# Half of the score spreads moved from SP's queue to GpSimd's, first values loaded earlier, mixing weights built earlier

## The chip, the cores and the metric

The kernel runs on one core of a Trainium2 chip. A core has a matrix engine (TensorE, PE in the profile), three engines for elementwise work (VectorE or DVE, ScalarE or ACT, GpSimd or POOL), SyncE (SP), which here only issues transfers, and 16 DMA engines that carry out the transfers of all queues. The metric is the time of one launch in microseconds of the device.

## What is computed

The reference is a talking-heads attention followed by two feed-forward blocks, in float32. Cut to what matters:

```python
# batch 2, 12 heads, 448 positions, head size 64
scores = q @ k^T / 8                                 # per head
scores = einsum('bhij,hg->bgij', scores, w_pre)      # mix the heads
attn   = softmax(scores)                             # over j
attn   = einsum('bhij,hg->bgij', attn, w_post)       # mix again
x      = (attn @ v), heads side by side              # 896 x 768
x = (h * clip(h + 3, 0, 6) / 6) @ w_out    with h = x @ w_in     # 768 -> 2048 -> 768
x = (P(h) / Q(h)) @ w_out2                 with h = x @ w_in2    # P cubic, Q quadratic
```

## The kernel before

**Tiles.** The 896 query rows are cut into eight chunks (`chunks`, four for each batch), six of them of 120 rows and two of 88 (the last of a batch, carried as 100). A chunk's rows form 12 groups of 10 rows (10 groups in the short chunks), and a step of the main loop (line 506) takes two groups. Scores are made for one head at a time with the chunk's rows on the partitions (`scores`, line 214, matrix product at L225). A mix over heads needs the heads on the partitions: for each group, 5 rows times 12 heads make 60 partitions, and two such halves lie at partitions 0 and 64. So each head's scores, once copied from PSUM into a staging tile (`stg`, five buffers, L230), are rearranged within the core by DMA into the tile `full` of the chunk (two buffers). This is the **spread**: two transfers a head of 60 rows of 448 floats (105 KB), 24 a chunk (line 197, issue at L201). For chunks 0 and 1 all heads are staged first (`stage`, `stage1`), and the spreads go by group instead of by head, 24 a chunk as well (`spread_group`, line 204, L206), so that the first group can be mixed before the last has come.

**A step** of the main loop does, for pair m of groups: `premix(m)`, the first mix on TensorE (M, L245), a row maximum on VectorE (L251) and the exponential on ScalarE (L253); `postmix(m - 2)`, the second mix (A, L287), which also normalizes, as its weights `wr` were divided by the row sums; the scores of the next chunk, two head pairs in each of the steps 0 to 2 (`SST`); the product of attention and values of the chunk before, X (L310, `av_unit`), two head pairs in each of the steps 3 to 5, or three in each of the steps 3 and 4 where the chunk itself has five steps (`AVST`; `AVLAST` in the last chunk); the copies; and `norm(m)` (line 258), where VectorE inverts the row sums and GpSimd multiplies them into the weights `wr` (L263). A wr is read by the `postmix` two steps later.

**The order** is the program's own: from line 436 on the schedule is written by hand, and each engine and each DMA queue works off its instructions in the order of the code. All DMAs but two go through SP's queue. It holds, in this order, the loads of keys and queries, chunk 0's spreads by group (L444), chunk 1's (from step 3 of chunk 0, L510), the first four loads of values (step 4, L513), and then for each chunk the 24 spreads in the order of the heads and the loads of values. There are four buffers for values (`vraw`), each for a pair of heads. `av_unit` issues the load four pairs ahead when it has emitted the products of a pair (L314); so pairs 4 and 5 of a chunk are loaded when pairs 0 and 1 have been used, in the same chunk's turn. Each transfer signals its landing by a semaphore, of which SP's queue uses eight in turn.

`build_mix` (line 179) makes, on GpSimd, the weights of both mixes (`wp`, `wq`) from the tiny loaded matrices.

**After the attention** come the two feed-forward blocks. Their weights are loaded, unpacked and split into two parts on ScalarE and VectorE ahead of the matrix products (h, y, acc at L331 to L333), which take three passes each. The first products h begin within the last chunk's steps (L566).

Of the kernel before, what the change touches and what calls it, by code (L numbers as in the profile page):

```python
# [22 lines left out]
HR = GR // 2  # L23
# [23 lines left out]
def fused_kernel(  # L47
# [15 lines left out]
    nc = tc.nc  # L63
# [49 lines left out]
    def load_q(C):  # L113
        ns = chunks[C][3] * GR
        t = front.tile([128, NP, CH], F32, tag="qraw", bufs=3, name=f"qraw{C}")
        nc.sync.dma_start(out=t[:, :, :ns], in_=q[C, :, :, :ns])
        qraw[C] = t

    def load_k(b, hp):
        if hp == 0:  # L120
            keys[b] = front.tile([128, NP, S], F32, tag="keys", bufs=2, name=f"keys{b}")
        nc.sync.dma_start(out=keys[b][:, hp], in_=k[b, :, hp])

    def load_v(C, hp):
        if C < len(chunks) - 1:
            t = att.tile([JP, 2, JC * D], F32, tag="vraw", bufs=4, name=f"vraw{C}_{hp}")
            nc.sync.dma_start(out=t, in_=v[chunks[C][0], hp])
            vraw[(C, hp)] = t
# [22 lines left out]
    for i, w in enumerate((w_pre, w_post)):  # L151
        for a in range(0, 128, 64):
            nc.sync.dma_start(
                out=wrep[a : a + HP, i, :], in_=w[None, :, :].to_broadcast([HR, H, H])
# [16 lines left out]
    def load_ab():  # L171
        nc.sync.dma_start(out=pa, in_=p_a.partition_broadcast(128))
        nc.sync.dma_start(out=pb, in_=p_b.partition_broadcast(128))

    def build_ab():
        nc.scalar.activation(out=pb, in_=pb, func=AF.Abs)
        nc.vector.tensor_scalar(out=pa, in0=pa, scalar1=-1.0, scalar2=None, op0=ALU.mult)

    def build_mix():
        w = wp[:, :HP].rearrange("p (i g) -> p i g", g=H)  # L180
        nc.gpsimd.tensor_tensor(
            out=w,
            in0=mask[:, :, None].to_broadcast([128, HR, H]),
            in1=wrep[:, 0, None, :].to_broadcast([128, HR, H]),
            op=ALU.mult,
        )
        nc.gpsimd.tensor_scalar(out=w, in0=w, scalar1=float(D) ** -0.5, scalar2=None, op0=ALU.mult)
        nc.gpsimd.tensor_tensor(
            out=wq,
            in0=wrep[:, 1, :, None].to_broadcast([128, H, HR]),  # L190
            in1=mask[:, None, :].to_broadcast([128, H, HR]),
            op=ALU.mult,
        )
# [2 lines left out]

    def spread(C, h, st):
        n = chunks[C][3]
        for a in range(2):
            to = full[C][64 * a : 64 * a + HP].rearrange("(i h) g s -> h i g s", h=H)[h]  # L200
            nc.sync.dma_start(out=to[:, :n], in_=st[a * HR * n : (a + 1) * HR * n])  # L201

    def spread_group(C, g, st):
        n = chunks[C][3]
        for a in range(2):
            nc.sync.dma_start(  # L206
                out=full[C][64 * a : 64 * a + HP, g, :],
                in_=st[a * HR * n : (a + 1) * HR * n].rearrange("(i g) h s -> g i (h s)", g=n)[g],
            )
# [4 lines left out]
    def scores(C, hp, tag="sc", st=None):  # L214
        n = chunks[C][3] * GR
        b = chunks[C][0]
        if hp == 0:
            full[C] = att.tile([128, MG, S], F32, tag="full", bufs=2, name=f"full{C}")
        sc = [ps.tile([128, 512], F32, tag=tag, bufs=BUFS[tag], name=f"sc{C}_{2 * hp + i}") for i in range(2)]
        far = st is None  # L220
        if far:
            st = front.tile([CH, 2, S], F32, tag="raw", bufs=5, name=f"stg{C}_{hp}")
        for i in range(2):
            o = slice(i * D, i * D + D)
            nc.tensor.matmul(  # L225
                sc[i][:n, :S], lhsT=qraw[C][o, hp, :n], rhs=keys[b][o, hp], start=True, stop=True
            )

        def take(i, copy):
            copy(out=st[:n, i], in_=sc[i][:n, :S])  # L230
            if far:
                spread(C, 2 * hp + i, st[:, i])

        return [lambda copy: take(0, copy), lambda copy: take(1, copy)]
# [4 lines left out]
    def premix(m):  # L239
        C, g = pairs[m]  # L240
        mt = [ps.tile([128, 512], F32, tag="M", bufs=BUFS["M"], name=f"M{m}_{a}") for a in range(2)]
        for a in range(2):
            for c in range(2):
                o = slice(64 * a, 64 * a + HP)
                nc.tensor.matmul(  # L245
                    mt[a][64 * c : 64 * c + 64, :S], lhsT=wp[o], rhs=full[C][o, g + c, :], start=True, stop=True
                )
        st = att.tile([128, 8], F32, tag="st", bufs=5, name=f"st{m}")
        e = att.tile([128, 2, S], F32, tag="e", bufs=3, name=f"e{m}")
        for a in range(2):  # L250
            nc.vector.tensor_reduce(out=st[:, a : a + 1], in_=mt[a][:, :S], op=ALU.max, axis=AX.X, negate=True)  # L251
        for a in range(2):
            nc.scalar.activation(  # L253
                out=e[:, a], in_=mt[a][:, :S], func=AF.Exp, bias=st[:, a : a + 1], accum_out=st[:, 2 + a : 3 + a]
            )
        epx[m] = (e, st)
# [162 lines left out]
    def load_units(i):  # L419
        while ucur[0] < len(units) and ucur[0] <= i:  # L420
            load_unit(units[ucur[0]])
            ucur[0] += 1
# [17 lines left out]
    for hp in range(NP):  # L440
        ev = scores(0, hp, "sc" if hp % 3 else "M", stage[:, 2 * hp : 2 * hp + 2])
        ev[0](acopy)
        ev[1](vcopy)
    for g in range(chunks[0][3]):  # L444
        spread_group(0, g, stage)
    build_mix()

    for hp in range(FIRST):
        ev = scores(1, hp, st=stage1[:, 2 * hp : 2 * hp + 2])
# [53 lines left out]
    for C, (b, r0, n, G) in enumerate(chunks):  # L503
        nxt = C + 1 if C + 1 < len(chunks) else None
        G //= 2
        for s in range(G):
            if C and C + 2 < len(chunks) and s == (3 if C == 1 else 0):
                load_q(C + 2)
            if C == 0 and s == 3:
                for g in range(chunks[1][3]):  # L510
                    spread_group(1, g, stage1)
                XL = xp.tile([128, KD, NT], F32R, tag="xl", name="xl")
            if C == 0 and s == 4:  # L513
                for i in range(4):
                    load_v(0, i)
            if C == 2 and s >= 3:
                load_k(1, 2 * s - 6)
                load_k(1, 2 * s - 5)
            if C == 2 and s == 1:
                load_ab()  # L520
            if C == 3 and s == 0:
                build_ab()
            premix(m)
            for p in later:
                p()
            later.clear()
            sc, xs = [], []
            if m >= LAG:
                postmix(m - LAG)
            if nxt is not None and not C:  # L530
                if s < NP - FIRST:
                    sc += scores(nxt, FIRST + s, st=stage1[:, 2 * FIRST + 2 * s : 2 * FIRST + 2 * s + 2])
            elif nxt is not None:
                for hp in range(NP):
                    if SST[hp] == s:
                        sc += scores(nxt, hp)
            if C:
                for i, t in enumerate(AVST[G] if nxt is not None else AVLAST):
                    if t == s:
                        xs += av_unit(C - 1, 2 * i + 1)  # L540
            for p in sc[:-1]:
                p(vcopy)
            if m >= LAG:
                at_evac(m - LAG, acopy)
            for p in sc[-1:]:
                p(acopy)
            for p in xs[::2]:
                p()
            later += xs[1::2]
            norm(m)  # L550
            if C == PRE and s == LATE - 1:
                front.release()
                pools["late"] = tc.alloc_tile_pool(name="late", bufs=1, side="right", reuse_waits="tile")
                load_units(1)
                wpieces = (p for u in units[:4] for p in split_pieces(u))
            if C == PRE and s == G - 1:
                pieces(1)
            if C > PRE:
                pieces(2)
            if C > PRE and s == 1:  # L560
                load_vs()
            if C > PRE and s == 2:
                load_units(2)
            if nxt is None and s >= 3:
                if s == 3:
                    h100 = gemm1(0, 0, ps.tile([128, 512], F32, tag="sc", bufs=BUFS["sc"], name="h1_0_0"))  # L566
                for _ in range(3):
                    next(h100)
            m += 1

    C = len(chunks) - 1
# [315 lines left out]
```

## Time and profile before

| | |
|---|---|
| median of 3 runs | 764.01 us (761.32 to 765.96) |
| the profiled execution | 762.19 us, its span 760.4 us |
| TensorE busy | 666.9 us, 88% of the span |
| VectorE, ScalarE busy | 502.7 us (66%), 383.8 us (50%) |
| GpSimd busy | 32.1 us (4%) |
| mean granted clock of TensorE | 0.942 |
| DMA queue of SP | 122.94 MB, 50.7% of 16 engines' span |

The span runs from the first to the last instruction; the execution's own time has some 1.8 us around it. Times in rows are microseconds from the start of the span unless marked ns. PE is a matrix product, PEld a weight load beside it; SPq is SP's sequencer, which issues transfers. `full<-stg` is a transfer or instruction that writes the tile `full` and reads `stg`. An arrow to the left behind an idle time names what ended it. The granted clock is given as a share of full speed: 1.00 is 2.4 GHz, 0.50 is 1.2 GHz.

### The profile page before, as it was taken

To read this page: it belongs to the slowest core of one execution; us is meant where nothing else is said; L and a number is where in the kernel's file an instruction comes from. 1 tells how busy PE (TensorE), PEld (TensorE's weight loads), DVE (VectorE), ACT (ScalarE), POOL (GpSimd) and SP (SyncE) were. 2 spreads that over 40 slices of the span, in tenths; PEclk is the share of its full clock that TensorE was granted. 3 is DMA by queue.
4 is the path that set the end of the run, shared out by engine and by line. 5 is a ranking of instruction groups with operands and counts; after the bars stand their busy time and mean duration, and the time that the engine had idled before them with its cause. 6 is when DMAs were issued, how large, how long until landed. Compare 5 with 4: busy or idle time off the path is not lost.

```text
span 760.4 us, 16385 instructions
## 1 busy us (share of the span) xinstructions
PE 666.9 (88%) x6682; PEld 558.0 (73%) x6682; DVE 502.7 (66%) x860; ACT 383.8 (50%) x701; POOL 32.1 (4%) x67
## 2 busy tenths in 40 slices
PE   8966485565749599999999999999999999999998
PEld 2434253343436468988988888888999999999997
DVE  4442162434435265989999855553999899999991
ACT  4643162435445364555565333322766667669861
POOL 1100010001000042000000000000000000000000
PEclk9996696868788899999999999999999999999999
DMA  5343528343442674756665533332765766574622
GB/s 176 123 146 119 147 94 201 121 123 131 118 148 93 198 215 130 229 170 215 213 194 187 160 110 112 111 126 103 253 214 201 240 221 249 168 257 149 200 92 84
DMA packets 77055, 124.35 MB, mean 164 GB/s; under 512 B 6804, under 2 KB 57268, under 8 KB 76980
## 3 DMA queue, kind: packets, MB, share of 16 engines
q1 hardware_dynamic: 76692, 122.94, 50.7%
q8 instruction: 53, 0.87, 0.5%
q10 hardware_dynamic: 288, 0.37, 0.1%
q14 instruction: 22, 0.18, 0.1%
HBM read 84.24 MB, written 19.27 MB: 136 GB/s over the span
## 4 chain that ended last, share of the span: by engine, by line
PE 79%; DMA 11%; SPq 3%; ACT 3%; DVE 2%; issue 1%; POOL 0%; ACTq 0%; DVEq 0%; POOLq 0%
PE h L331 10%; PE h L332 10%; PE h L333 10%; DMA vraw<-in_v_dram 6%; PE M L245 5%; PE X L310 5%; PE y L331 5%; PE y L333 5%; PE acc L331 5%; PE acc L332 5%; PE acc L333 5%; PE y L332 5%; PE sc L225 4%; PE A L287 3%; DMA full<-stage 3%; ACT e L253 2%
## 5 line engine op out<-in xcount | busy, mean ns | idle before, releaser
L331 PE MATMUL h<-xh,wh 128*128 128x512 f32 (+1 forms) x384 | 140.4, 366 | 0.0
L332 PE MATMUL h<-xl,wh 128*128 128x512 f32 (+1 forms) x384 | 140.3, 365 | 0.0
L333 PE MATMUL h<-xh,wl 128*128 128x512 f32 (+1 forms) x384 | 139.2, 363 | 0.0
L251 DVE TENSOR_REDUCE st<-M 128x1 f32<-128x448 f32 x92 | 53.8, 620 | 114.7 <-PE M L245 111.5
L310 PE MATMUL X<-at,vraw 120*64 120x120 f32 (+1 forms) x672 | 49.1, 313 | 79.4 <-DMA vraw<-in_v_dram 79.3
L310 PEld LDWEIGHTS X<-at,vraw 120*64 120x64 f32 x672 | 43.8, 169 | 81.6 <-DMA vraw<-in_v_dram 72.0
L253 ACT ACTIVATE e<-M,st 128x448 f32<-128x448 f32 x92 | 57.6, 630 | 55.7 <-DVE st L251 55.5
L331 PEld LDWEIGHTS h<-xh,wh 128*128 128x128 f32 x384 | 72.2, 188 | 8.2 <-issue 0.2
L333 PEld LDWEIGHTS h<-xh,wl 128*128 128x128 f32 x384 | 72.2, 188 | 8.0
L332 PEld LDWEIGHTS h<-xl,wh 128*128 128x128 f32 x384 | 72.3, 188 | 6.6
L406 ACT ACTIVATE wh<-wf 128x768 fp32r<-128x768 f32 (+1 forms) x52 | 42.5, 818 | 60.6 <-PE y L332 48.2
L379 ACT ACTIVATE wf<-wraw 128x768 f32<-128x768 f32 (+1 forms) x56 | 49.5, 884 | 46.6 <-DVE wl L407 44.1
L333 PE MATMUL y<-gh,wl 128*128 128x384 f32 x192 | 70.7, 368 | 0.0
L331 PE MATMUL y<-gh,wh 128*128 128x384 f32 x192 | 70.5, 367 | 0.0
L407 DVE TENSOR_TENSOR wl<-wf,wh 128x768 fp32r<-128x768 f32 (+1 forms) x52 | 48.0, 923 | 33.9 <-ACT wh L406 33.9
L332 PE MATMUL y<-gl,wh 128*128 128x384 f32 x192 | 70.0, 364 | 0.0
L245 PE MATMUL M<-full,wp 60*64 60x448 f32 x368 | 62.6, 596 | 6.9 <-ACT e L253 6.6
L287 PEld LDWEIGHTS A<-wr,e 60*56 60x56 f32 x2944 | 50.4, 130 | 24.3 <-issue 19.2
L383 DVE SCALAR_TENSOR_TENSOR wf<-wraw,icst,wf 128x768 int32<-128x768 int32 (+1 forms) x56 | 55.2, 987 | 1.0
L387 DVE SCALAR_TENSOR_TENSOR wf<-wraw,icst,wf 128x768 int32<-128x768 int32 (+1 forms) x56 | 55.2, 985 | 0.7
L287 PE MATMUL A<-wr,e 60*56 60x60 f32 x2944 | 52.1, 218 | 1.0 <-ACT at L295 1.0
L323 ACT ACTIVATE xh<-X 128x240 fp32r<-128x240 f32 (+1 forms) x24 | 8.7, 365 | 80.5 <-PE X L310 80.5
(96 smaller groups left out, 1182.4 us busy)
## 6 DMA issues: line engine op xcount, KB each, us to landing
wraw<-in_moe_w_out_dram SPq DMA_DIRECT2D x28, 768.0 KB
wraw<-in_moe_w_in_dram SPq DMA_DIRECT2D x22, 768.0 KB
vraw<-in_v_dram SPq DMA_DIRECT2D x42, 240.0 KB
full<-stg SPq DMA_DIRECT2D x96, 105.0 KB
wpre<-in_moe_w_in_dram SPq DMA_DIRECT2D x10, 768.0 KB
w2h<-wh SPq DMA_DIRECT2D x16, 384.0 KB
w2l<-wl SPq DMA_DIRECT2D x16, 384.0 KB
ws<-w2h SPq DMA_DIRECT2D x16, 384.0 KB
```

The costliest lines, as they stand in the source:

```text
L245: nc.tensor.matmul(mt[a][64 * c : 64 * c + 64, :S], lhsT=wp[o], rhs=full[C][o, g + c, :], start=True, stop=True)
L251: nc.vector.tensor_reduce(out=st[:, a : a + 1], in_=mt[a][:, :S], op=ALU.max, axis=AX.X, negate=True)
L253: nc.scalar.activation(out=e[:, a], in_=mt[a][:, :S], func=AF.Exp, bias=st[:, a : a + 1], accum_out=st[:, 2 + a : 3 + a])
L287: nc.tensor.matmul(av[64 * c : 64 * c + JH, r, jc, :, a * HR : a * HR + HR], lhsT=e[o, a, j : j + JH], rhs=wr[o, a], start=True, stop=True,)
L310: nc.tensor.matmul(X[hh % 2 * D : hh % 2 * D + D, hh % 4 // 2, :n], lhsT=vs[:, jc, :], rhs=at[C][:, jc, hh, :n], start=(jc == 0), stop=(jc ...
L331: nc.tensor.matmul(o, lhsT=wh, rhs=mh, start=first, stop=False)
L332: nc.tensor.matmul(o, lhsT=wh, rhs=ml, start=False, stop=False)
L333: nc.tensor.matmul(o, lhsT=wl, rhs=mh, start=False, stop=last)
L379: nc.scalar.activation(out=w, in_=hw.bitcast(F32), func=AF.Copy, scale=2.0**-112)
L383: nc.vector.scalar_tensor_tensor(out=wi, in0=hw, scalar=icst[:, 0:1], in1=wi, op0=ALU.bitwise_and, op1=ALU.bitwise_or)
L387: nc.vector.scalar_tensor_tensor(out=wi, in0=lw, scalar=icst[:, 1:2], in1=wi, op0=ALU.logical_shift_right, op1=ALU.bitwise_or)
L407: nc.vector.tensor_tensor(out=lv, in0=w, in1=hv.bitcast(F32), op=ALU.subtract)
```

## The change

Of the two transfers that spread a head's scores (or a group's), the first stays in SP's queue and the second goes into GpSimd's. `build_mix` is emitted before the spreads of chunk 0 instead of after them. The first four loads of values are emitted in step 1 of chunk 0, behind its `premix`, instead of in step 4 ahead of it.

```diff
@@ -196,14 +196,14 @@
 
     def spread(C, h, st):
         n = chunks[C][3]
-        for a in range(2):
+        for a, eng in enumerate((nc.sync, nc.gpsimd)):
             to = full[C][64 * a : 64 * a + HP].rearrange("(i h) g s -> h i g s", h=H)[h]
-            nc.sync.dma_start(out=to[:, :n], in_=st[a * HR * n : (a + 1) * HR * n])
+            eng.dma_start(out=to[:, :n], in_=st[a * HR * n : (a + 1) * HR * n])
 
     def spread_group(C, g, st):
         n = chunks[C][3]
-        for a in range(2):
-            nc.sync.dma_start(
+        for a, eng in enumerate((nc.sync, nc.gpsimd)):
+            eng.dma_start(
                 out=full[C][64 * a : 64 * a + HP, g, :],
                 in_=st[a * HR * n : (a + 1) * HR * n].rearrange("(i g) h s -> g i (h s)", g=n)[g],
             )
@@ -441,9 +441,9 @@
         ev = scores(0, hp, "sc" if hp % 3 else "M", stage[:, 2 * hp : 2 * hp + 2])
         ev[0](acopy)
         ev[1](vcopy)
+    build_mix()
     for g in range(chunks[0][3]):
         spread_group(0, g, stage)
-    build_mix()
 
     for hp in range(FIRST):
         ev = scores(1, hp, st=stage1[:, 2 * hp : 2 * hp + 2])
@@ -510,9 +510,6 @@
                 for g in range(chunks[1][3]):
                     spread_group(1, g, stage1)
                 XL = xp.tile([128, KD, NT], F32R, tag="xl", name="xl")
-            if C == 0 and s == 4:
-                for i in range(4):
-                    load_v(0, i)
             if C == 2 and s >= 3:
                 load_k(1, 2 * s - 6)
                 load_k(1, 2 * s - 5)
@@ -521,6 +518,9 @@
             if C == 3 and s == 0:
                 build_ab()
             premix(m)
+            if C == 0 and s == 1:
+                for i in range(4):
+                    load_v(0, i)
             for p in later:
                 p()
             later.clear()
```

## Rows read from the trace of the kernel before

**Rows 1.** Busy time by stretch: length, then PE, PEld, DVE, ACT, POOL; clock, DMA share, GB/s.

```profile
60.00:290.00 230.00, 151.50 (x3528) 106.43 (x3526) 93.06 (x227) 99.58 (x228) 23.64 (x44) 0.82 0.48 140
290.00:760.40 470.40, 466.73 (x2472) 428.78 (x2470) 383.29 (x573) 257.02 (x416) 3.41 (x3) 1.00 0.54 177
```

**Rows 2.** Waits before 300 us: us in total, times, longest us.

```profile
PE X L310 <- DMA vraw<-in_v_dram: 79.3, 7, 14.0
PE M L245 <- ACT e L253: 6.6, 3, 4.6
...
DVE stg L230 <- DMA full<-stg: 16.2, 2, 15.9
```

**Rows 3.** Chain of waits, 136 to 165 us: start us, us, what.

```profile
145.02 0.60 SPq L201
...
150.15 8.05 DMA vraw<-in_v_dram
```

**Rows 4.** SP's queue in order of time: start us, us, line, transfer, count.

```profile
10.21 38.68 SPq L206 DMA_DIRECT2D full<-stage  x48
...
49.05 4.49 SPq L127 DMA_DIRECT2D vraw<-in_v_dram  x4
...
138.04 12.02 SPq L201 DMA_DIRECT2D full<-stg  x14
```

**Rows 5.** SP's issues by tile: ns min/median/max, first and last start us.

```profile
L201 SPq DMA_DIRECT2D full<-stg x144: 712/732/1016, 54.8 to 254.4; - x144
...
L127 SPq DMA_DIRECT2D vraw<-in_v_dram x42: 324/330/1053, 49.1 to 274.5; - x42
```

**Rows 6.** DMA, 141 to 149 us, then 150 to 158: packets, MB, share; 40 slices.

```profile
q1 hardware_dynamic: 560, 0.93, 32.4%
...
DMA  3333339539998999986979999987633333322324
...
q1 hardware_dynamic: 798, 1.40, 67.5%
```

**Rows 7.** TensorE in order of time, 158 to 175 us and 210 us: start us, us.

```profile
158.25 3.47 PE L310 MATMUL X<-at,vraw 120*64 120x120 f32 x32 [13.99 <-DMA vraw<-in_v_dram]
...
161.64 1.77 PE L245 MATMUL M<-full,wp 60*64 60x448 f32 x8
...
166.37 0.98 PE L245 MATMUL M<-full,wp 60*64 60x448 f32 x8
167.18 1.02 PE L287 MATMUL A<-wr,e 60*56 60x60 f32 x64
...
170.67 1.06 PE L287 MATMUL A<-wr,e 60*56 60x60 f32 x64
...
210.38 1.86 PE L310 MATMUL X<-at,vraw 120*64 120x120 f32 x32
```

**Rows 8.** VectorE and GpSimd, 165 to 169 us: start us, us, idle before.

```profile
165.72 1.69 DVE L230 COPY stg<-sc 120x448 f32<-120x448 f32 x3 [0.42 <-PE sc L225]
...
167.86 0.39 POOL L263 TENSOR_TENSOR wr<-wq,st 128x120 f32<-128x120 f32 x1 [22.29 <-DVE st L261]
```

**Rows 9.** Groups by line: busy us, mean ns, idle before it.

```profile
L404 POOL TENSOR_TENSOR wl<-wf,wh 128x768 fp32r<-128x768 f32 x4 | 7.4, 1843 | 0.3
...
L407 DVE TENSOR_TENSOR wl<-wf,wh 128x768 fp32r<-128x768 f32 (+1 forms) x52 | 48.0, 923 | 33.9 <-ACT wh L406 33.9
```

**Rows 10.** First two chunks, GpSimd and TensorE in order of time: start us, us.

```profile
26.99 0.39 POOL L263 TENSOR_TENSOR wr<-wq,st 128x120 f32<-128x120 f32 x1 [4.02 <-DVE st L261]
...
23.24 0.43 PE L287 MATMUL A<-wr,e 60*56 60x60 f32 x12
...
34.03 0.43 PE L287 MATMUL A<-wr,e 60*56 60x60 f32 x12
...
39.22 1.77 PE L225 MATMUL sc<-keys,qraw 64*120 64x448 f32 x8
...
58.73 3.40 PE L310 MATMUL X<-at,vraw 120*64 120x120 f32 x32 [8.58 <-DMA vraw<-in_v_dram]
```

## The prediction

> **What bounds the kernel now.** I read four views in this order. First the busy time by stretch [rows 1]: from 290 us to the end TensorE is busy 466.73 of 470.40 us at a clock of 1.00, and the change touches nothing there. Between 60 and 290 us it is busy 151.50 of 230 us at a mean clock of 0.82, so what can be won lies there, in the attention. Then TensorE's waits [rows 2]: of its idle time before 300 us, 79.3 us in 7 waits of up to 14.0 us are products X (attention times values) waiting for the load of vraw; another 6.6 us, one wait of 4.6 among them, are mixes M behind a late exponential. Third, the chain through one of the seven [rows 3]: from 145.02 us it runs along SP's spreads at L201, at 150.15 us it changes to a vraw load, and that takes 8.05 us to land. So the wait has two halves: 5 us in which the load stands behind spreads in SP's queue, and 8 us of transfer.
>
> Fourth, both halves by themselves. **The queue:** SP issues 24 spreads a chunk at a median of 732 ns where a vraw load takes 330 [rows 5], and with the gaps 0.81 to 0.86 each: 14 of them take 12.02 us, and chunks 0 and 1 take 38.68 us for 48 [rows 4]. **The transfer:** where only spreads run, their packets take 32.4% of the 16 DMA engines, which is 5.2 engines' work [rows 6], 560 packets or 9.3 spreads of 60 rows in 8 us, 0.86 us each. So a spread keeps about five engines busy, and these serve hardly faster than SP issues. When the vraw loads come, the line of 40 slices goes from 3 to 9 tenths and falls back to 3 before the loads are in [rows 6]: eleven engines have finished and five still work off the spreads ahead of the loads.
>
> **The change, part by part.** Twelve of a chunk's 24 spreads go to GpSimd's queue; SP saves 12 x 0.81 = 9.7 us a chunk. TensorE's step with scores is 3.5 us long (A to A, 167.18 to 170.67 [rows 7]), four heads fall into it, and SP's four remaining issues, 3.2 us, fit in. So SP is no longer behind when the X of a chunk begin, and the load for head pair 4, which waits for the X of pair 0 to free its buffer, goes out at once. It has two steps less half an X, 7.0 - 0.9 = 6.1 us, until it is needed. Its transfer was 8.05 us behind the backlog; with fewer spreads ahead I take 7 us, and leave 1 us of each of the seven waits: 79.3 - 7 = **72.3 us less**. The five-step chunk has less room than that, which the 1 us is to cover on the mean.
>
> The wait of 4.6 us at M stems from the same backlog: just before it VectorE's copy of scores waits 15.9 us for a staging buffer whose spread has not landed [rows 2]. **4.6 less**. After each wait TensorE also works at the low level, 1.2 GHz: at 158 us X takes 3.47 us where it takes 1.86 later, and M 1.77 where it takes 0.98 [rows 7], 2.4 us here. I take 2 for each of seven: **14 less**. In all 90.9 us.
>
> Against it stand GpSimd's costs. No row shows a DMA issued by GpSimd; call its price p. The nearest row from below is SP's own issue of this transfer, 0.73 us [rows 5]. On one and the same subtraction GpSimd takes 1843 ns where VectorE takes 923 [rows 9], 2.0 times as long; by that p would be 1.46 at most. I take **1.0**: between the two, nearer to SP's row, which is the same transfer. GpSimd's slowest instruction, 1.84 us, is the outer bound. The Trainium skill (DMA: Bandwidth & Descriptors, Latency and other measured facts) gives about 1 us to the first byte on this path against 0.6 on SP's; by that alone the sum would be the same.
>
> GpSimd's queue is in order, and behind the spreads stands wr, the weights that each second mix A needs. In a step with scores the first copy is done at about 166.4 us, wr runs at 167.86 for 0.39, and the A that reads it starts at 170.67 [rows 7, 8]: 2.4 us to spare. With four spreads ahead of it, wr ends at 166.4 + 4p + 0.4, so at p = 1.0 it is 0.1 us late; the next two steps each add 4p + 0.4 - 3.5 = 0.9. That is 1.9 us a chunk, in general 12p - 10.1, over six chunks: **11.4 more**.
>
> In the first two chunks it is coarser. Chunk 0's twelve run from 10.2 to 22.2 us, and wr for step 0 comes at 22.6, in time for its A at 23.24 [rows 10]. Chunk 1's twelve stand ahead of step 3's wr. They begin when the third wr is through, 27 us, and end at 39; the A of step 3, at 34.03 before, follows at 39.4, and the scores of chunk 2, at 39.22 before, at some 42.4: **3 more**. These scores were held up by spreads before too, so little of the 5 us shows.
>
> **The early load of the first values** moves four issues of SP, 330 ns each, from 49.05 us [rows 4] to behind chunk 0's twelve, about 20 us, and ahead of chunk 1's twelve, which wait for the copies of step 2's scores anyway. So nothing queues behind them for long. Its gain, the 8.58 us that the X of 58.73 us waits [rows 10], is one of the seven waits and counted there. If chunk 1's halves on SP came 1.5 us later, the 39.4 us of GpSimd would cover it. **The mixing weights ahead of the spreads** cost nothing: they must be there before the first M, and GpSimd would otherwise make them twelve spreads later, some 12 us.
>
> Sum: 762.2 (this execution: span 760.4 and 1.8 around it) - 90.9 + 11.4 + 3 = 685.7. The median of the runs stands 1.8 us above this execution, so **687**.
>
> **Rivals.** (a) *The same five engines.* If GpSimd's spreads run on the engines that SP's use, the transfers don't get faster. A chunk's 24 spreads need 24 x 0.86 = 20.6 us of them and TensorE asks for them within three steps, 10.5 us. When the load for pair 4 is issued, about half of SP's twelve are still ahead of it, sharing the engines with as many of GpSimd's, some 10 us; it lands about 5 us after it is needed instead of 1. With 4.5 us in each of six chunks, 27 in all, the time is 714. For it speaks that a transfer of the same shape takes five engines now [rows 6]; against it that no row says which five GpSimd would take. The Trainium skill speaks against the change here (DMA: Bandwidth & Descriptors, Rules for kernel authors): spreading DMAs over SP, ACT and GpSimd gives no bandwidth and only saves issue time. The same page (Why a DMA increments its semaphore by 16 and not by 1) has GpSimd's transfers begin at an engine that moves on from one to the next, where SP's take the lowest-numbered. No row here decides between the two.
>
> (b) *A dearer issue*, p = 1.5: 12p - 10.1 = 7.9 us a chunk, 47, and 9 in chunk 1; with the 90.9 that leaves 34.5 of gain, 729.
>
> (c) *GpSimd's queue becomes the bound, and the kernel slower.* In each chunk TensorE then waits at A for wr, three steps in a row. The loss 6 x (12p - 10.1) + 3 + 12(p - 1) meets the 90.9 at p = 1.91; from there it decides. At p = 2.2 it is 115, and the time 788. For it speaks that wr has 2.4 us of room and that GpSimd has taken up to twice another engine's time; against it that 1.91 is above every row of GpSimd's and 2.6 times SP's own issue.
>
> (d) *It does nothing that shows:* the loads stay late for another reason, as SP's queue waits for X to free buffers anyway, and 764 stands. Against it: in the chain of rows 3 the load is preceded by spreads alone, not by an X.
>
> **How the numbers follow.** My forecast 0.60 (665 to 705: p from 0.73 to 1.2, and a rest of 0 to 1 us at each wait), (a) 0.13, (b) 0.13, (c) 0.10, (d) 0.04. Faster by more than 0.5%, about the least that a measurement of this kernel tells from no change, is the forecast with (a) and (b): 0.86; the same 0.04; slower 0.10. The low end, 665, is p = 0.73 with no wait left; the high end, 735, takes in (a) and (b). What stays out is (c), (d) and the tails of the others, 0.2.
>
> **What would show it.** Right: TensorE's waits for vraw fall from 79.3 us to under 15; SP's line shows 12 spreads a chunk with the vraw load right after an X; GpSimd has 96 DMA issues of about 1.0 us each; TensorE's clock between 60 us and the end of the attention is near 1.00, and the stretch in which TensorE hardly waits any more starts near 214 us instead of 290 [rows 1]; A waits for wr some 2 us a chunk. Rival (a): the DMA share where spreads run alone stays at a third, and X still waits several us a chunk. (b) and (c): GpSimd's issues take 1.5 us or 2 us and more, and A waits for wr in three steps of every chunk. The forecast is wrong if p is over 1.3, or if another engine (VectorE, which copies, reduces and normalizes in each step) sets the step as soon as TensorE no longer waits.

## The result, and the profile after

The changed kernel takes 727.09 us (median of 4 runs, 725.2 to 730.83) against 764.91 for the kernel before beside it (4 runs): a ratio of 0.952, 95% interval 0.947 to 0.957. That is faster and within the range, but the gain is 37.8 us where some 77 was forecast. The profiled execution took 725.2 us, its span 723.4, 37.0 less than the one before.

The first view again is busy time by stretch, columns as in [rows 1]; the second row cuts the attention at 255 us, behind its last long wait:

```profile
60.00:290.00 230.00, 184.17 (x3744) 134.76 (x3735) 119.24 (x262) 114.77 (x250) 61.64 (x104) 0.90 0.61 164
...
60.00:255.00 195.00, 149.17 (x3531) 103.57 (x3523) 90.33 (x220) 97.68 (x222) 58.95 (x102) 0.88 0.61 161
```

The attention is shorter, but not dense: from 60 to 255 us TensorE is idle for 46 of 195 us, at a mean clock of 0.88. The waits before 300 us say what for (us in total, times, longest us); they answer to [rows 2]:

```profile
PE X L310 <- DMA vraw<-in_v_dram: 41.0, 7, 9.1
...
PE A L287 <- POOL wr L263: 4.7, 2, 4.3
...
PE M L245 <- ACT e L253: 3.2, 4, 1.2
PE M L245 <- DMA full<-stage: 3.0, 2, 2.2
```

X still waits 41.0 us for vraw, where 7 was forecast. A waits for wr almost only once. So GpSimd's side went better than forecast and SP's worse. The issues by tile (ns min/median/max; first and last start) show both, against [rows 5]:

```profile
L201 SPq DMA_DIRECT2D full<-stg x72: 712/802/2561, 47.4 to 214.3; - x72
L201 POOL DMA_DIRECT2D full<-stg x72: 573/582/632, 47.7 to 212.2; - x72
L206 SPq DMA_DIRECT2D full<-stage x24: 721/1124/3073, 10.1 to 45.2; - x24
L206 POOL DMA_DIRECT2D full<-stage x24: 573/593/792, 10.8 to 39.6; - x24
```

An issue costs GpSimd 0.58 us, less than SP. SP's own issues of the same transfers have grown: by head from 0.73 to 0.80 us in the median, by group from 0.74 to 1.12, and the longest of all from 1.02 to 3.07. What that does to a value load is seen in the two queues in order of time, first GpSimd's and then SP's, while one chunk's scores are spread (start us, us):

```profile
110.33 2.43 POOL L201 DMA_DIRECT2D full<-stg  x4 [11.47 <-DMA qraw<-in_q_dram]
...
113.95 2.43 POOL L201 DMA_DIRECT2D full<-stg  x4 [0.78 <-DVE stg L230]
...
117.40 2.55 POOL L201 DMA_DIRECT2D full<-stg  x4 [0.61 <-DVE stg L230]
```

```profile
110.06 15.31 SPq L201 DMA_DIRECT2D full<-stg  x12
125.46 11.20 SPq L127 DMA_DIRECT2D vraw<-in_v_dram  x6
```

GpSimd issues its half of a head as soon as the copy is done, the last four at 117.40 to 119.95. SP's halves of the same four heads, ready just as early, go out until 125.4: the single issues there take 2.22, 1.83, 0.96 and 0.94 us. SP is held by its issues, not by data. Nor do its eight semaphores hold it: the one that each of these four issues takes in its turn had its earlier landing complete 3.7 to 4.7 us before. TensorE in order of time beside it:

```profile
119.12 2.68 PE L310 MATMUL X<-at,vraw 120*64 120x120 f32 x48
...
123.60 1.04 PE L310 MATMUL X<-at,vraw 120*64 120x120 f32 x16
132.83 3.47 PE L310 MATMUL X<-at,vraw 120*64 120x120 f32 x32 [8.19 <-DMA vraw<-in_v_dram]
136.23 1.77 PE L245 MATMUL M<-full,wp 60*64 60x448 f32 x8
```

The first 16 of the products at 119.12 use head pair 0; they end at 120.2 and free the buffer that pair 4's load needs. Had SP kept pace with GpSimd, it would have been through by then; it issues that load at 125.46. TensorE wants the values at 124.6 and gets them at 132.8. The chain of waits through that place has the same three pieces (start us, us):

```profile
124.88 0.48 SPq L201
...
125.46 7.23 DMA vraw<-in_v_dram
...
132.83 3.47 PE X L310 x32
```

**Each wait taken apart.** From single products and issues of the trace I worked out, for pair 4 of a chunk, how long after its buffer came free the load was issued (late), how long from the issue to the X that used it (transit), and how long TensorE had other work from the freeing on (room). Late plus transit less room is the wait. Means over X of the first six chunks, in us:

| kernel | late | transit | room | wait |
|---|---|---|---|---|
| before | 11.5 | 7.6 | 7.3 | 11.8 |
| after | 5.1 | 8.0 | 6.3 | 6.8 |
| forecast for after | 0 | 7 | 6.1 | 1 |

Transit and room were forecast nearly right. The lateness was to vanish, and only halved.

### The profile page after: what moved, and what is told of

It is laid out like the page before. It is cut to its first block, busy times and chain, and to the rows that moved or that the text cites. A ratio compares the mean times of both kernels' runs of the same rounds, so it can differ in the third digit from the quotient of the medians.

```text
span 723.4 us, 16553 instructions
## 1 busy us (share of the span) xinstructions
PE 663.3 (92%) x6682; PEld 555.0 (77%) x6682; DVE 502.5 (69%) x860; ACT 383.4 (53%) x701; POOL 88.6 (12%) x163
## 4 chain that ended last, share of the span: by engine, by line
PE 84%; DMA 9%; issue 3%; ACT 1%; SPq 1%; POOL 1%; DVE 1%; POOLq 0%; ACTq 0%; DVEq 0%
PE h L331 11%; PE h L332 11%; PE h L333 11%; DMA vraw<-in_v_dram 6%; PE y L331 5%; PE y L333 5%; PE acc L331 5%; PE acc L332 5%; PE acc L333 5%; PE y L332 5%; PE X L310 5%; PE M L245 5%; PE sc L225 5%; PE A L287 4%; DMA full<-stage 2%
## 5 line engine op out<-in xcount | busy, mean ns | idle before, releaser
L253 ACT ACTIVATE e<-M,st 128x448 f32<-128x448 f32 x92 | 57.5, 629 | 60.3 <-DVE st L251 60.3
L310 PE MATMUL X<-at,vraw 120*64 120x120 f32 (+1 forms) x672 | 46.4, 302 | 41.0 <-DMA vraw<-in_v_dram 41.0
L310 PEld LDWEIGHTS X<-at,vraw 120*64 120x64 f32 x672 | 41.2, 160 | 43.0 <-issue 41.3
L245 PE MATMUL M<-full,wp 60*64 60x448 f32 x368 | 56.5, 621 | 6.2 <-ACT e L253 3.2
L201 POOL DMA_DIRECT2D full<-stg x72 | 42.4, 589 | 83.9 <-DVE stg L230 52.7
```

Source lines behind the costliest of these rows:

```text
L245: nc.tensor.matmul(mt[a][64 * c : 64 * c + 64, :S], lhsT=wp[o], rhs=full[C][o, g + c, :], start=True, stop=True)
L253: nc.scalar.activation(out=e[:, a], in_=mt[a][:, :S], func=AF.Exp, bias=st[:, a : a + 1], accum_out=st[:, 2 + a : 3 + a])
L310: nc.tensor.matmul(X[hh % 2 * D : hh % 2 * D + D, hh % 4 // 2, :n], lhsT=vs[:, jc, :], rhs=at[C][:, jc, hh, :n], start=(jc == 0), stop=(jc ...
```

## The experiments

All ratios are against the kernel before, run on the same chip; it took 762.6 to 763.9 us in these sessions. The edits are shortened to what matters: `...` stands for lines or arguments left out, and remarks behind `#` are not in the code. Two readings of the late loads stood against each other after the result. P: GpSimd's transfers share engines with SP's, whose transfers therefore crawl and hold SP's issues, and the loads stand behind them. Against it: the loads are late whatever queue they stand in, or GpSimd's issuing as such slows SP's.

### What is left without GpSimd's queue

```diff
-        for a, eng in enumerate((nc.sync, nc.gpsimd)):
+        for a, eng in enumerate((nc.sync, nc.sync)):      # in spread and spread_group
```

> The changed kernel with both halves of every spread on SP, so that only the early load of the first values and the mixing weights ahead of the spreads are left of the change. If the gain is GpSimd's queue nearly alone, as the two undone parts (2 and 3 us, each inside the noise) say: 755 to 765 us, X waits still 65 us or more, SP's issues of spreads back at a median of 0.73 us. Rival (the parts need each other, or the early load carries a large share of the gain): under 750 us.

763.58 us (12 runs), ratio 1.001 (0.9986 to 1.0033). X waits in six places instead of seven and M, behind two kinds of releaser, for 13.4 us instead of 6.6:

```profile
PE X L310 <- DMA vraw<-in_v_dram: 72.2, 6, 14.2
PE M L245 <- ACT e L253: 10.1, 3, 8.1
PE M L245 <- DMA full<-stage: 3.3, 4, 1.5
```

So the early load and the early weights give nothing that shows by themselves: what X gains there M loses. The gain comes with GpSimd's queue. This run is also the cleanest look at what that queue does to SP, as no X is near in the first 50 us. SP's queue there, both halves on SP (start us, us):

```profile
10.40 19.32 SPq L206 DMA_DIRECT2D full<-stage  x24
29.77 2.39 SPq L127 DMA_DIRECT2D vraw<-in_v_dram  x4
32.27 21.36 SPq L206 DMA_DIRECT2D full<-stage  x24
```

and in the changed kernel:

```profile
10.10 15.74 SPq L206 DMA_DIRECT2D full<-stage  x12
25.88 3.01 SPq L127 DMA_DIRECT2D vraw<-in_v_dram  x4
30.48 16.02 SPq L206 DMA_DIRECT2D full<-stage  x12
```

Half the spreads take 81% and 75% of the time: 0.81 and 0.89 us each alone, 1.31 and 1.34 beside GpSimd's. The forecast had counted 0.81.

### The two small parts undone, one at a time

The loads of the first values back at their old place:

```diff
-            if C == 0 and s == 1:      # behind premix
+            if C == 0 and s == 4:      # ahead of premix
                 for i in range(4):
                     load_v(0, i)
```

> The changed kernel with the first four loads of values back in step 4 of chunk 0, behind chunk 1's spreads. If the early load is worth its old wait (8.6 us before the X of 58.7 us), a wait of 5 to 9 us comes back at chunk 1's first X and the time is 731 to 736; if what follows swallows it, the time stays within 725 to 729.

728.92 us, ratio 0.956 (0.951 to 0.961): 2 us from the changed kernel, inside the intervals. And the weights behind the spreads again:

```diff
-    build_mix()
     for g in range(chunks[0][3]):
         spread_group(0, g, stage)
+    build_mix()
```

> The changed kernel with the mixing weights made behind chunk 0's spreads again. GpSimd then makes them when its twelve issues are through, at about 20 us instead of 8 to 9, and the first M starts at about 21 us instead of 13.8: 6 to 8 us more, 733 to 735, if nothing later swallows it; 727 if it does.

730.42 us, ratio 0.957 (0.951 to 0.963). The waits show what the move prevents:

```profile
PE M L245 <- POOL wp L187: 7.6, 1, 7.6
```

but most of these 7.6 us were swallowed later; the time differs by 3 us, and that is not resolved.

### The second half on ScalarE's queue

```diff
-            eng.dma_start(out=to[:, :n], in_=st[a * HR * n : (a + 1) * HR * n])
+            x, y = to[:, :n], st[a * HR * n : (a + 1) * HR * n]
+            if a:
+                held_s.append((x, y))
+            else:
+                nc.sync.dma_start(out=x, in_=y)
...                                       # at the end of the step:
             later += xs[1::2]
+            for x, y in held_s:
+                nc.scalar.dma_start(out=x, in_=y)
+            held_s.clear()
```

> The second half of every chunk's spreads by head goes to ScalarE's queue instead of GpSimd's (issued at the end of the step; the first two chunks' spreads by group stay as in the changed kernel). Theory E (GpSimd's transfers run on other DMA engines than SP's, and that is where the gain comes from): ScalarE's spreads sit on the same five engines as SP's, the DMA share where spreads run alone stays near a third (0.33 to 0.40), X still waits 70 us or more in all, and the time is 745 to 785, the upper end from ScalarE's own 12 issues of 0.73 us a chunk. Theory I (only SP's issue time counts, whoever takes the other half): X waits some 41 us as in the changed kernel, and the time is 727 to 745.

745.69 us, ratio 0.976 (0.972 to 0.980). X waits only 6.9 us, for another reason than either side had named: ScalarE was late. Its exponentials stand behind its own issues, and these behind landings. The group of the exponentials (busy us, mean ns, idle before and what ended it):

```profile
L257 ACT ACTIVATE e<-M,st 128x448 f32<-128x448 f32 x92 | 57.6, 630 | 115.5 <-DMA full<-stg 57.5 <-DVE st L255 36.0 <-DVE stg L234 21.7
```

M then waits 36.5 us for e in all. But one thing is plain here. In stretches in which both queues only carry spreads the DMA share (the last but one column) is that of SP alone [rows 6]:

```profile
120.00:125.00 5.00, 3.91 (x80) 1.77 (x78) 3.20 (x7) 2.63 (x6) 0.39 (x1) 1.00 0.34 119
125.00:130.00 5.00, 1.54 (x8) 0.43 (x6) 1.69 (x3) 0.56 (x2) 0.00 (x0) 1.00 0.33 120
```

In the changed kernel, in the chunk shown above (the third row is the wait of X, for later):

```profile
112.00:116.00 4.00, 4.00 (x88) 2.24 (x86) 3.41 (x8) 3.01 (x7) 3.11 (x7) 1.00 0.58 152
116.00:120.00 4.00, 4.00 (x98) 2.42 (x95) 3.21 (x8) 2.92 (x8) 3.17 (x7) 1.00 0.72 172
128.00:132.00 4.00, 0.00 (x0) 0.00 (x0) 0.00 (x0) 0.00 (x0) 0.00 (x0) 0.50 0.91 224
```

ScalarE's spreads run on the engines that SP's use, five of 16; GpSimd's bring other engines in. The Trainium skill (DMA: Bandwidth & Descriptors, Rules for kernel authors) holds that spreading DMAs over SP, ACT and GpSimd gives no bandwidth; the trace agrees for SP with ScalarE and disagrees for SP with GpSimd. The rule of the Trainium skill (DMA: Bandwidth & Descriptors, Why a DMA increments its semaphore by 16 and not by 1) that GpSimd's transfers begin at an engine that moves on fits the shares of 0.58 and 0.72.

The packets themselves, counted in the trace:

```
kernel, stretch     queue    bytes  packets per us  mean ns  engines busy
before, 141-149     SP        1792            64.6       79           5.1
after,  113-119     SP        1792            43.3       90           3.9
after,  113-119     GpSimd    5376            19.3      335           6.5
```

SP's spreads lose a third of their packets per us, while GpSimd's come in packets of three rows. The Trainium skill (DMA: Bandwidth & Descriptors, Queues, rings and completion order) says that an engine takes turns between its queues packet by packet; with that rule a small packet of SP would wait for a large one of GpSimd on each engine that both use, which is what P assumes. The counts fit it.

### The value loads taken out of SP's queue

On ScalarE's queue, at the end of the step:

```diff
-        load_v(...)                       # in av_unit
+        held_v.append(...)
...
             later += xs[1::2]
+            for args in held_v:
+                load_v(*args, eng=nc.scalar)
+            held_v.clear()
```

> The changed kernel with the loads of values by pair (from pair 4 of chunk 0 on) in ScalarE's queue, issued at the end of the step, instead of in SP's behind the spreads. Theory P (the loads are late because they stand behind held spreads in SP's queue): they go out at the end of the step and land in 3 to 5 us, the X waits fall under 15 us, time 690 to 705. Theory Q (the engines are busy whatever the queue): a load still takes 7 us or more to land, the X waits stay at 25 us or more, time 712 to 727.

730.72 us, ratio 0.957 (0.954 to 0.961), as the changed kernel, and above what either theory said. The waits show that it was half a success, X between the two:

```profile
ACT e L253 <- DMA vraw<-in_v_dram: 23.6, 4, 8.0
PE X L310 <- DMA vraw<-in_v_dram: 19.5, 11, 4.6
```

X waits half as long, but ScalarE's issues wait for earlier landings and hold the exponentials. On GpSimd's queue there is no such work behind them but wr. Of the 42 loads 38 go there; the first four stay with SP:

```diff
-        load_v(...)                       # in av_unit
+        load_v(..., eng=nc.gpsimd)
```

> The changed kernel, with the 42 loads of vraw moved from SP's queue to GpSimd's, in front of GpSimd's spreads of the same step. Theory P (SP's issues are held because its packets alternate with GpSimd's larger ones; the load's lateness is mostly the time it stands behind held spreads): GpSimd's issues stay near 0.6 us and are not held, the load goes out as soon as X frees its buffer, TensorE's waits of X for vraw fall from 41 us to under 18; GpSimd's queue gets some 4 us longer per chunk, so A waits for wr 5 to 20 us; time 700 to 722. Rival B (the load is late because the engines that carry it are full, whatever queue it stands in): X waits stay at 30 us or more, time 722 to 735.

739.56 us, ratio 0.970 (0.966 to 0.973): slower than both expectations. X's waits fell to 26.0 us, between them. GpSimd in order of time, in the third chunk:

```profile
123.49 2.39 POOL L201 DMA_DIRECT2D full<-stg  x4 [0.64 <-DVE stg L230]
...
127.44 1.15 POOL L127 DMA_DIRECT2D vraw<-in_v_dram  x2 [1.14 <-DMA full<-stg]
```

The load goes out 1.2 us after its buffer is free, and is in 10.1 us later. On the mean it is 1.1 late, its transit 9.4, its room 6.2: P's lateness is gone as it said, but the load now lands behind GpSimd's own spreads (one issued at 125.30 lands at 136.15, the load at 137.54), and spreads end up late too (in this kernel's chain the `full<-stg` that SP issues at 129.84 takes 12.65 us). A load that is issued in time is not a load that lands in time; that was P's mistake. X is not what makes this run slower than the changed kernel: it waits 15.0 us less. M's waits are 23.6 us in all instead of 6.2, and TensorE is busy 677.1 us instead of 663.3, at a mean clock of 0.935 instead of 0.956.

### More of the spreads on GpSimd

All from chunk 2 on:

```diff
-            eng.dma_start(out=to[:, :n], in_=st[a * HR * n : (a + 1) * HR * n])
+            nc.gpsimd.dma_start(out=to[:, :n], in_=st[a * HR * n : (a + 1) * HR * n])
```

> From chunk 2 on all 24 spreads of a chunk go through GpSimd's queue, SP keeps only loads there. Theory P (on the engines that both queues use, GpSimd's packets of 5376 bytes take turns with SP's of 1792, so SP's spreads crawl, SP's issue is held, and the loads of values stand behind it): without spreads of SP the X waits fall from 41 us to under 15, A waits for wr about 4 us a chunk (eight issues of 0.58 us and 0.4 in a step of 3.5), time 695 to 712. Theory Q (the loads are slow because the DMA engines as a whole are busy, whatever queue the spreads stand in): X waits stay at 30 us or more, A's waits come on top, time 727 to 745.

712.91 us, ratio 0.935 (0.931 to 0.939), just above P's range. The waits before 300 us:

```profile
PE A L287 <- POOL wr L263: 31.6, 18, 4.7
...
PE X L310 <- DMA vraw<-in_v_dram: 0.7, 2, 0.4
```

With no spread in SP's queue each pair-4 load goes out 0.04 us after its buffer is free, in every chunk, and X no longer waits. GpSimd has twice as many issues by head as in the changed kernel, still at 0.58 us each, and SP's issue of a value load is at a median of 328 ns: this speaks against GpSimd's issuing as such slowing SP's. In exchange wr is late, three times a chunk; this slows TensorE and gives the loads more room, so the run does not price P alone. Three quarters on GpSimd, the odd heads' first halves as well:

```diff
+            eng = nc.gpsimd if h % 2 else eng
             eng.dma_start(out=to[:, :n], in_=st[a * HR * n : (a + 1) * HR * n])
```

> From chunk 2 on GpSimd's queue takes 18 of a chunk's 24 spreads (both halves of every second head), SP 6. Theory P (on the engines that both use, SP's spreads get one packet of 1792 bytes for each of GpSimd's of 5376, are held, and hold the loads of values behind them): SP has half as many to get through, X waits fall from 41 to 10 to 20 us, A waits for wr 8 to 15 us (six issues of 0.58 and 0.4 are 3.9 us in a step of 3.5), time 705 to 715. Theory H (GpSimd's issuing as such slows SP's issue): with half as much again on GpSimd's queue SP's issues take longer than the 0.80 us median of the changed kernel, X waits stay near 40 us, time 725 or more.

711.62 us, ratio 0.935 (0.929 to 0.940), the fastest beside the run with all, and not told apart from it. Late 0.04, transit 9.3, room 8.0: the wait is down to 1.4 us a chunk. The issues by tile:

```profile
L202 POOL DMA_DIRECT2D full<-stg x108: 573/582/632, 46.7 to 198.7; - x108
L202 SPq DMA_DIRECT2D full<-stg x36: 712/732/1990, 47.9 to 194.5; - x36
```

SP's issues by head are back at a median of 732 ns, from 802 in the changed kernel, beside half as many again of GpSimd's: by this too it is not GpSimd's issuing that slows them. SP's six spreads a chunk are issued before X begins. A waits 18.8 us for wr, X 10.4.

### Smaller packets on GpSimd's queue

```diff
+            x, y = to[:, :n], st[a * HR * n : (a + 1) * HR * n]
+            for u in range(1 + a):
+                w = S // (1 + a)
+                eng.dma_start(out=x[:, :, u * w : u * w + w], in_=y[:, u * w : u * w + w])
```

> The changed kernel, with each of GpSimd's spreads by head cut into two transfers of half rows (224 floats): the same bytes, twice the issues. Theory P says that the size of GpSimd's packets decides how slowly SP's move: if a packet still takes three rows, it is 2688 bytes instead of 5376, SP's spreads get a larger share and SP's issue of spreads by head goes back to a median under 0.78 us with a maximum under 2 us; X waits fall to 15 to 30 us. GpSimd's 24 issues a chunk of 0.58 us make A wait for wr some 30 us, as with all spreads on GpSimd; time 725 to 740. Theory B (only the bytes on the engines count): SP's issues and the X waits stay as they were, 41 us, and the A waits come on top: 750 or more.

725.4 us, ratio 0.949 (0.945 to 0.954). This didn't decide. GpSimd's packets became 4480 and 1792 bytes, not half of 5376; SP's median issue by head came down to 764 ns from 802, and its packets, at 44 per us (112 to 122 us), were about as many as the 43 in the table; X's waits fell to 4.9 us, below both expectations, but with twice the issues A waited 36.5 us for wr, which gives every load room. That packet size is what holds SP is thus argued from the counts, not shown.

### What limits once the queues don't

All spreads on GpSimd, and wr on ScalarE instead (last chunk left):

```diff
+        if pairs[m][0] < len(chunks) - 1:
+            for a in range(2):
+                nc.scalar.activation(out=wr[:, a]..., in_=wq..., func=AF.Copy, scale=st[:, 6 + a : 7 + a])
+        else:
             nc.gpsimd.tensor_tensor(out=wr, ...)
```

> All spreads from chunk 2 on in GpSimd's queue, and wr (all chunks but the last) made on ScalarE by two multiplications of 128x60 instead of on GpSimd behind the spreads. If GpSimd's queue order is what A waits for in the version with all spreads on GpSimd (31.6 us in 18 waits), these waits fall under 5 us, ScalarE spends some 0.4 us more a step, and the time is 680 to 692 against 712.9. If A then waits for something else as long (ScalarE's or VectorE's turn in the step), the time stays above 700.

725.82 us, ratio 0.952 (0.947 to 0.956): the 31.6 us of A are gone and the time is worse by 13 us. The waits and, below, busy time by stretch with the DMA share as the last but one column:

```profile
PE M L245 <- DMA full<-stg: 33.5, 9, 8.3
...
PE X L317 <- DMA vraw<-in_v_dram: 5.7, 5, 3.1
```

```profile
121.00:125.00 4.00, 3.20 (x100) 2.51 (x92) 1.81 (x5) 2.47 (x6) 2.72 (x6) 1.00 0.98 234
125.00:129.00 4.00, 1.04 (x16) 0.81 (x16) 0.00 (x0) 0.83 (x3) 1.45 (x3) 0.98 1.05 200
129.00:133.00 4.00, 0.00 (x0) 0.00 (x0) 0.00 (x0) 0.00 (x0) 0.00 (x0) 0.50 1.03 217
```

All 16 engines are full for 12 us (shares of 0.98 to 1.05), and M waits for the last spreads. To see whether that was this one queue's doing, both edits together, three quarters on GpSimd and wr on ScalarE:

```diff
+            eng = nc.gpsimd if h % 2 else eng        # in spread
...
+                nc.scalar.activation(out=wr[:, a]..., in_=wq..., func=AF.Copy, scale=st[:, 6 + a : 7 + a])
```

> GpSimd issues 18 of a chunk's 24 spreads (odd heads both halves), and wr is made by ScalarE in two activations instead of by GpSimd (last chunk left as it was), so that A no longer waits behind GpSimd's issues: 18.8 us of waits of A are there to be won against the run without the second edit. If transfers are the limit by now (the spreads and loads of a chunk landing late however they are issued, as in the run with all spreads on GpSimd and wr on ScalarE): the waits come back at X for vraw or at M for full, 15 to 35 us together, and the time is 705 to 728. If that run lost its time only because one queue held all spreads: X and M together wait under 12 us, and the time is 690 to 704.

714.57 us (6 runs), ratio 0.936 (0.933 to 0.938), in the first branch: A's 18.8 us are gone, and X's waits have doubled:

```profile
PE X L318 <- DMA vraw<-in_v_dram: 21.0, 7, 5.1
...
PE M L246 <- ACT e L254: 10.6, 4, 7.7
```

One wait of 7.7 us for e, in ScalarE's order, came with the extra work there. In chunks 1 to 5 the loads are 0.2 us late, but take 9.9 from issue to use. While TensorE waits for one, the engines are nearly full:

```profile
120.00:124.00 4.00, 1.92 (x84) 1.62 (x76) 1.80 (x5) 2.47 (x6) 0.88 (x2) 1.00 0.92 205
124.00:127.00 3.00, 0.00 (x0) 0.00 (x0) 0.00 (x0) 0.00 (x0) 0.00 (x0) 0.92 0.93 203
```

So by these two runs the next limit, at some 712 us, is the transfers themselves: a chunk's spreads and its value loads meet in the same few us. What would spread them over the chunk (a fifth buffer for values) was not tried.

## Why the prediction was right or wrong

The signs held: faster, by SP's queue being relieved, through shorter waits of X. Half of the size did not come. The sum's terms against the profiled executions, in us:

| term | forecast | measured |
|---|---|---|
| X waits for vraw | -72.3 | -38.3 |
| M waits for e | -4.6 | -3.4 |
| slow clock behind each wait | -14 | -3.6 (all of TensorE's busy time; see the clock below) |
| wr late, six chunks | +11.4 | about 0 |
| A in chunk 1 | +3 | +4.7 |
| M waits for chunk 0's spreads by group | 0 | +3.0 |
| rest | 0 | +0.6 |
| sum | -76.5 | -37.0 |

**The step that failed** is "four heads fall into it, and SP's four remaining issues, 3.2 us, fit in. So SP is no longer behind". It took SP's price of 0.81 us from a trace in which SP had its engines to itself, and kept it beside a second queue. In the chunk shown the last four spreads took 6.2 us instead, and the load that was to go out "at once" was 5.3 us late, on the mean of six chunks 5.1. Transit was taken as 7 and was 8.0, room as 6.1 and was 6.3. The lateness alone makes 30.4 of the 34.0 us that are missing at X. That the second queue is what slows SP's issues is shown by the runs with both halves on SP and with more on GpSimd; how it does so, by packets that take turns, is argued from counts.

**The clock** gave nothing, where 14 us were forecast. Six long waits remain of seven, and the X behind each still takes 2.6 to 3.5 us, against 1.86 at full speed. The X at 132.83 takes 3.47 us and the M behind it 1.77, the very figures of [rows 7]; the row of 128 to 132 us above, in the wait, has the clock at 0.50, the lower of its two levels. The forecast tied its 14 us to waits that would vanish; they shortened instead. And two stretches at the low level are new, one behind waits of M in chunk 0, one around the wait of A in chunk 1 (the kernel before has 1.00 there):

```profile
22.10:28.90 6.80, 6.80 (x81) 3.83 (x80) 3.18 (x7) 3.06 (x10) 0.39 (x1) 0.50 0.46 148
39.20:46.00 6.80, 5.36 (x138) 4.12 (x140) 1.16 (x2) 2.13 (x5) 2.05 (x5) 0.50 0.57 141
```

In all stretches at the low level before 300 us TensorE was busy 34.2 of 88.8 us before and 38.1 of 61.2 after: less time there, but no less work done at half speed. Where the 3.6 us of busy time come from stays open.

**GpSimd's price** was 0.58 us, below the lower bound of 0.73: the nearest row, SP's issue, was no floor. With 0.58 the forecast's own 12p - 10.1 is negative, and wr is indeed in time outside chunk 1. There the wait has the place forecast, A following at 40.64 where 39.4 was forecast, but its size agrees by luck. Twelve issues of 0.58 us from the 27 us of the forecast would have ended at 34 and the wr behind them 0.4 later, and the A of 34.03 would hardly have waited. The third wr, ahead of them, came at 30.77 instead, and issues behind waited up to 1.64 us for the landing of earlier spreads:

```profile
31.37 4.62 POOL L206 DMA_DIRECT2D full<-stage  x8 [0.21 <-issue]
...
38.46 1.71 POOL L206 DMA_DIRECT2D full<-stage  x3 [1.64 <-DMA full<-stage]
```

The scores of chunk 2 come at 45.5 instead of 42.4, as the SP halves are slower too.

**Rival (a)** had the right kind of trouble and the wrong reason. Its five engines are disproved (DMA share 0.58 and 0.72, not a third), yet its half-served queue ahead of the load is what happened: it put 4.5 us more on each of six waits, 27 in all, and 34.0 came. Its 714 missed by 13 us all the same: 7 of them are X's, and the rest M's and A's waits in the first two chunks for the most part, as the 10.4 us that the clock did not give and the 11.4 that wr did not cost cancel by chance. (b) and (c) fell with the price; (d) fell too, but the run with all spreads on SP shows that it holds for the two small parts, which the forecast had costed at nothing beyond that one wait.

**The early load** does take the wait from the first X, 8.58 us in [rows 10]; undone in the changed kernel it costs 2 us that can't be told from none.

## What to carry to other kernels

A price of an issue holds for the load on the queue in which it was measured: before halving a queue's work, ask which engines the other half will run on, and price the remaining half beside it. Take a late load apart into late, transit and room; here the second queue halved the first, and lengthened the second a little (7.6 to 8.0 us). When a wait is mended and the time stays, look at the DMA share in that stretch: where it is near 1, as in the last two runs here, the transfers themselves are what to spread out. And where a gain of the clock is counted behind a wait, look for the new waits that the change makes: here two of them took it back.

## What the hardware showed that was not expected

- GpSimd issues a 60-row spread in 0.58 us, and SP in 0.73; of the single loads of values GpSimd takes 0.55, SP 0.33.
- SP's issue stretches from 0.73 to as much as 3.07 us when GpSimd's queue works beside it; in the chunk shown, for spreads whose data had been there for up to 5 us and whose semaphores were free.
- Two queues can share five engines (SP and ScalarE, DMA share 0.33) or not (SP and GpSimd, 0.58 to 0.72), for the same transfers. GpSimd's packets held three rows, 5376 bytes, where SP's held one, 1792.
- An engine that computes pays for issuing transfers with more than the issue: ScalarE stood idle 57.5 us for landings of earlier spreads with 72 of them in its queue.
